# A four-layer transformer stack on one core: another layout of the rows stored in DRAM, and one order for the way into the output stage of both attention layers

## The chip, the core and the metric

The kernel runs on one core of a Trainium2 chip. The metric is the time of one execution on the device in microseconds, the median of several runs. TensorE multiplies matrices (PE in the profile; its weight loads, which overlap it, are PEld), VectorE is DVE, ScalarE is ACT, GpSimd is POOL. SyncE (SP) computes nothing: it issues the DMA transfers, one after the other. Weights and activations live in SBUF, sums of matmuls in PSUM, and what does not have to stay on the core goes to DRAM.

## The reference

Four layers on x of 2048 tokens by 576 features, in bfloat16: attention (A), MLP (B), A, B, each with a residual and a layer norm ahead of it.

```python
def _A_ref(x, wqkv, wo):
    H = 32; Dh = D // H                                  # 32 heads of 18
    qkv = (x @ wqkv).reshape(B, S, 3, H, Dh).transpose(2, 0, 3, 1, 4)
    q, k, v = qkv[0], qkv[1], qkv[2]
    phi = lambda t: jnp.where(t > 0, t + 1, jnp.exp(t)) + 1e-6
    pq, pk = phi(q), phi(k)
    kv = jnp.einsum("bhsd,bhse->bhde", pk, v)
    z = jnp.einsum("bhsd->bhd", pk)
    num = jnp.einsum("bhqd,bhde->bhqe", pq, kv)
    den = jnp.einsum("bhqd,bhd->bhq", pq, z)[..., None] + 1e-6
    o = num / den
    return o.transpose(0, 2, 1, 3).reshape(B, S, D) @ wo

def _B_ref(x, w1, b1, w2, b2):
    h = _gelu(jnp.einsum("bsd,df->bsf", _layernorm(x), w1) + b1)   # F = 4608
    return jnp.einsum("bsf,fd->bsd", h, w2) + b2

x = x + _A_ref(_layernorm(x), A_wqkv, A_wo)
x = x + _B_ref(_layernorm(x), B_w1, B_b1, B_w2, B_b2)
x = x + _A_ref(_layernorm(x), A_wqkv, A_wo)
x = x + _B_ref(_layernorm(x), B_w1, B_b1, B_w2, B_b2)
```

The attention is linear: keys and values are summed into one small matrix per head before any query is used.

## The kernel before

The tokens are worked on in 16 tiles of 128 rows (t), four tiles to a chunk of 512 (c, and j within the chunk). The 32 heads lie in five groups g of 126, 126, 126, 126 and 72 columns. yT holds the normed rows turned: features on partitions, tokens along the row. TensorE's order in the attention layers is the order of the program text (`pe` chains every matmul to the one before), and each other engine works its own instructions in the order that the scheduler gave them.

**Rows through DRAM.** In layer 1 (an MLP), each tile that is finished is normed for layer 2 and goes two ways. VectorE turns its 32 x 32 blocks into `turned` (L258), SP stores a chunk of four such tiles in four pieces to `y_d` (L266) and loads it back as columns of `yT` (`land`, L283 for the first 512 features, L286 for the last 64). And the row itself is stored in `yrow_d` (L406), because layer 2 also multiplies rows by keys. The turning leaves the tokens of a chunk in another order: block i of 32 rows of each of the four tiles j. A reload for "row" t = 4c + i therefore gathers 32 rows from each of four stored tiles: `load_row` (L251) for the first 512 columns, and L292 in `land` for the last 64 columns (the tails, four loads to a chunk, kept in `v_ring`). `yrow_d` has the shape [4 chunks, 4 tiles j, 4 blocks i, 32, 576], so that a stored tile is one contiguous piece and a reloaded row tile is four pieces of 32 rows. On SP's queue, the last chunk's steps are: four stores to `y_d`, the reloads of rows 6 to 11, the two loads of `yT`, four tail loads, the reloads of rows 12 to 15, and the residual rows of layer 2. A transfer that needs another's data, or its semaphore, is not issued before that has landed, and everything behind it on SP's queue waits too.

**Layer 2's keys.** For each tile and each half of the columns, `k_half` (L610) computes keys from `yT`, a `q_proj` follows every second of them (L589), and three steps behind, `rows_by_keys` (L627) multiplies the reloaded row by the keys.

**The way into the output stage (both attention layers).** Behind the sums, TensorE does these pieces:

- `q_proj(g, c)`, L589: five matmuls for the queries of one group and chunk. ACT then makes exp and a shifted copy of the result (L468, L469), and VectorE a min and a max (L476, L480). With `defer=True` these four are put off until the returned function is called.
- `kv_wo(g)`, L736: the small matrix of a group times wo, into a PSUM pair (accB for even g, accA for odd). ACT or VectorE copies it to SBUF (L743, L741).
- `den_stage(c)`, L752 and L756: the denominators of a chunk; VectorE takes the reciprocal (L760), and `quad_stage(c)` spreads it over a masked tile (L767).
- `scale_stage(g, c)`, L777: one matmul that broadcasts the reciprocals to a group's rows; ACT copies it to SBUF (L779) and VectorE multiplies the queries by it (L780).
- `wo_stage(t)`, L789: ten matmuls for one tile into accA or accB in turn, then `residual` (L519) adds and stores the row. For the first four tiles the layer norm of the MLP follows, with statistics on ACT (L337, L344) and a transpose on TensorE (L425) some tiles later.

PSUM has eight banks: four single ones in the pool `ps_h` (queries, denominators, broadcasts, transposes), and the pairs accA and accB. A piece that needs a bank waits until the last reader of what stood there is done.

The two layers enter the stage in different orders. Layer 0: kv_wo 0, a q_proj, denominators of chunks 0 and 1, q_proj, kv_wo 1, q_proj, broadcasts 0 to 2, kv_wo 2 and 3, broadcasts 3 and 4, kv_wo 4, q_proj. Layer 2 (its kv_wo 0 and 1 are done earlier): a q_proj, denominators of chunk 0, the values' matrices (`kv_groups`), q_proj, kv_wo 2 and 3, broadcasts 0 to 2, kv_wo 4, q_proj, broadcasts 3 and 4, denominators of chunk 1. In the loop over the tiles, each tile does `wo_stage`, the next chunk's broadcasts (three behind j = 0, two behind j = 1), then a q_proj if one is left, and then the denominators of the chunk after the next (behind j = 2 in layer 0, j = 1 in layer 2).

Of the kernel before, what the change touches and what calls it, by code (L numbers as in the profile page):

```python
# [9 lines left out]
BF16 = mybir.dt.bfloat16  # L10
# [24 lines left out]
def build(tc, A_x, A_wqkv, A_wo, B_w1, B_b1, B_w2, B_b2, out, dbg=None, n_layers=4):  # L35
    nc = tc.nc
    dbg = dbg or {}
    with ExitStack() as ctx:
# [77 lines left out]
        yrow_d = dpool.tile([NCB, TPC, 4, 32, D], BF16, name="yrow_d")  # L116
# [132 lines left out]
        def load_row(t):  # L249
            row_of[t] = blk.tile([P, D], BF16, name="yrow", tag="blk")  # L250
            load = nc.sync.dma_start(out=row_of[t][:, 0:4 * P], in_=yrow_d[t // TPC, :, t % TPC, :, 0:4 * P])  # L251
            if t >= 6:
                behind(load, "turned" if t < NT - TPC else "landed")
# [20 lines left out]
        def land(now=False):  # L274

            for it in list(landing):
# [11 lines left out]
                if kind == "A":  # L288
                    if c == NCB - 1:
                        sp_last["landed"] = landed.ins.name  # L290
                    for i in range(4):
                        tail = nc.sync.dma_start(out=tails(c)[:, i, 0:64], in_=yrow_d[c, :, i, :, 4 * P:D])  # L292
                        behind(tail, "landed")
                    if c == NCB - 1:
                        for t in range(c * TPC, NT):
                            load_row(t)
# [8 lines left out]
        class LNPipe:  # L305
# [11 lines left out]
            def tick(self, transposes=1):  # L317
                land()
                for it in list(self.items):
# [63 lines left out]
                    elif st in (2, 3):  # L383
# [20 lines left out]
                        if it["kind"] == "A" and it["evac"] == "dma":  # L404
                            c, j = divmod(it["t"], TPC)
                            nc.sync.dma_start(out=yrow_d[c, j].rearrange("i r d -> (i r) d"), in_=y[:, 0:D])  # L406
# [122 lines left out]
        def layer_A(li, next_kind, pre_a1=None):  # L529
# [203 lines left out]
            def kv_wo(g):  # L733
# [6 lines left out]
                if g % 2 or (li > 0 and g == 4):  # L740
# [7 lines left out]
            def den_stage(c, after=None):  # L748
                dp = ps_h.tile([P, 512], F32, name="den_ps", tag="h")
# [25 lines left out]
            def scale_stage(g, c):  # L775
                bp = ps_h.tile([P, 512], F32, name="rden_ps", tag="h")
                pe(nc.tensor.matmul(bp[:], lhsT=head_bc[:, g, :], rhs=quad_rden[c][:, 0:CA], start=True, stop=True))  # L777
# [22 lines left out]
            if li == 0:  # L800
                kv_wo(0)
                q_proj(*q_left.pop(0))
                den_stage(0)
                quad_stage(0)
                den_stage(1)
                quad_stage(1)
                q_proj(*q_left.pop(0))
                kv_wo(1)
                q_proj(*q_left.pop(0))
                for g in range(3):  # L810
                    scale_stage(g, 0)
                kv_wo(2)
                kv_wo(3)
                for g in range(3, G):
                    scale_stage(g, 0)
                kv_wo(4)
                q_proj(*q_left.pop(0))
            else:
                phi = q_proj(*q_left.pop(0), defer=True)
                den_stage(0)  # L820
                quad_stage(0)
                phi(dve_after=dve_last["quad"])
                kv_groups((2, 3, 4))
                late = [q_proj(*q_left.pop(0), defer=True)]
                kv_wo(2)
                kv_wo(3)
                for g in range(3):
                    scale_stage(g, 0)
                kv_wo(4)
                late.append(q_proj(*q_left.pop(0), defer=True))  # L830
                for g in range(3, G):
                    scale_stage(g, 0)
                den_stage(1, after=dve_last["mult"])
                quad_stage(1, after=dve_last["mult"])
                for phi in late:
                    phi(after=act_last["copy"])
            for t in range(NT):
# [4 lines left out]
                for late in list(rden_of):  # L842
                    quad_stage(late, after=dve_last["sum"])
                if c + 1 < NCA:
                    for g in ((0, 1, 2), (3, 4), (), ())[j]:
                        scale_stage(g, c + 1)
                if q_left:
                    q_proj(*q_left.pop(0))
                if j == (1 if li > 0 else 2) and c + 2 < NCA:
                    den_stage(c + 2)  # L850
# [242 lines left out]
```

## Time and profile before

| | |
|---|---|
| three runs | 772.51, 772.74, 774.62 us; median 772.74 |
| the profiled execution | 774.99 us, its span 773.3 us, mean granted clock of TensorE 0.998 |
| TensorE busy | 762.7 us (99%) |
| ACT, VectorE, GpSimd busy | 339.2, 273.7 and 119.4 us |
| layer 0, up to the first matmul of the MLP | to 108.65 us |
| layer 1, up to the first keys of layer 2 | 108.65 to 390.4 us |
| layer 2, up to the first matmul of the MLP | 390.4 to 488.0 us |
| layer 3 | 488.0 us to the end |
| first wo of layer 0, first wo of layer 2 | 80.15 and 460.54 us |

The span runs from the first to the last instruction of the profiled execution. Busy time of TensorE counts a matmul from its start to a modelled end, and neighbours overlap: the distance from one piece's start to the next one's start is what a piece costs. In the lists of waits, an engine and a line stand on the left, and what it waited for on the right. In the windows, the granted clock is the share of TensorE's full clock that the throttle let through, and the DMA share is the mean busy share of the 16 DMA engines.

### The profile page before, as it was taken

The numbers are of one execution on the slowest core, as the hardware profiler recorded it, in microseconds if no ns is written. First come the engines' busy times: TensorE is split into PE (matmuls) and PEld (weight loads), VectorE is DVE, ScalarE is ACT, GpSimd is POOL, SyncE is SP. The second block draws the span as 40 slices with busy tenths as digits, with TensorE's granted clock in tenths as the row PEclk, the third lists the DMA queues.
The fourth block names the chain that finished last, engine by engine and source line by source line (L and its number), as shares of the span: only waits on it lengthen the run. The fifth ranks groups of instructions, "written<-read, shape, count | busy, mean of one in ns | idle before, by whom it ended". The sixth has DMA issues, their size and how long they took to land.

```text
span 773.3 us, 15726 instructions
## 1 busy us (share of the span) xinstructions
PE 762.7 (99%) x6554; PEld 493.8 (64%) x6554; DVE 273.7 (35%) x676; ACT 339.2 (44%) x755; POOL 119.4 (15%) x196
## 2 busy tenths in 40 slices
PE   9999999999999999999998999999999999999998
PEld 6776664675477457646776767547745764675476
DVE  7786864035114503401354678610140023000000
ACT  5887846304610650263055568461065026205600
POOL 4571412011100301200100004210030002002000
PEclk9999999999999999999999999999999999999999
DMA  8991473015401631320147006730141033011000
GB/s 261 275 287 46 154 250 89 24 57 155 129 24 63 180 81 47 108 66 16 53 124 189 25 1 209 252 81 9 38 124 51 16 123 83 8 31 54 2 8 24
DMA packets 80290, 73.83 MB, mean 95 GB/s; under 512 B 36698, under 2 KB 64858, under 8 KB 80218
## 3 DMA queue, kind: packets, MB, share of 16 engines
q1 hardware_dynamic: 80218, 72.82, 32.4%
q8 instruction: 51, 0.84, 0.5%
q14 instruction: 21, 0.17, 0.1%
HBM read 48.03 MB, written 24.77 MB: 94 GB/s over the span
## 4 chain that ended last, share of the span: by engine, by line
PE 94%; DMA 2%; DVE 2%; ACT 1%; issue 1%; POOL 0%; SPq 0%; ACTq 0%
PE m_ps L974 35%; PE h_ps L917 20%; PE hp_ps L917 16%; PE q_ps L589 5%; PE wo_ps L789 4%; PE k_ps L541 2%; PE k_ps L610 2%; PE k_ps L627 2%; PE v_ps L562 1%; DMA yT<-y_d 1%; PE m_half L974 1%; PE v_ps L559 1%; PE tp L425 1%; PE rden_ps L777 1%; ACT rden_bc L779 1%
## 5 line engine op out<-in xcount | busy, mean ns | idle before, releaser
L974 PE MATMUL m_ps<-w_sb,hT 128*128 128x288 bf16 x2232 | 274.8, 286 | 0.0
L974 PEld LDWEIGHTS <-hT 128*128 128x128 bf16 x2304 | 224.8, 98 | 59.8 <-issue 3.4
L917 PEld LDWEIGHTS <-w_sb 64*128 64x128 bf16 x2304 | 124.5, 94 | 136.5 <-issue 1.9
L917 PE MATMUL hp_ps<-yT,w_sb 64*128 64x512 bf16 x1152 | 178.0, 376 | 0.0
L917 PE MATMUL h_ps<-yT,w_sb 64*128 64x512 bf16 x1152 | 148.0, 376 | 0.0
L922 ACT COPY relay_sb<-relay_sb 128x1 f32<-128x1 f32 x144 | 28.5, 198 | 262.6 <-PE h_ps L917 220.0
L913 ACT ACTIVATE hT<-h_ps,b1T 128x512 bf16<-128x512 f32 x144 | 91.0, 683 | 44.4 <-PE h_ps L917 44.4
L376 POOL TENSOR_TENSOR ln_rstd<-ln_u,neg_half 128x1 f32<-128x1 f32 x64 | 35.9, 562 | 376.6 <-DVE ln_u L367 229.5
L913 ACT ACTIVATE hT<-hp_ps,b1T 128x512 bf16<-128x512 f32 x144 | 91.1, 692 | 0.0
L519 DVE TENSOR_TENSOR xbf<-m_ps,xo 128x576 bf16<-128x576 f32 x15 | 11.4, 758 | 212.1 <-PE m_ps L974 212.1
L519 DVE TENSOR_TENSOR xo<-m_ps,xo 128x576 f32<-128x576 f32 x16 | 12.1, 758 | 167.2 <-PE m_ps L974 167.2
L502 POOL TENSOR_TENSOR xo<-xo,b_bc 128x576 f32<-128x576 f32 x32 | 41.0, 1286 | 106.1 <-DMA xo<-x_d 66.0
L917 PE MATMUL h_ps<-yT,w_tail 64*128 64x512 bf16 x144 | 54.1, 376 | 0.0
L917 PE MATMUL hp_ps<-yT,w_tail 64*128 64x512 bf16 x144 | 54.1, 376 | 0.0
L589 PE MATMUL q_ps<-yT,wqkv_sb 128*126 128x512 bf16 (+1 forms) x200 | 50.8, 386 | 0.1
L789 PE MATMUL wo_ps<-kvwo,pq 126*128 126x288 bf16 (+1 forms) x320 | 43.1, 285 | 0.2 <-DVE xo L519 0.2
L917 PEld LDWEIGHTS <-w_tail 64*128 64x128 bf16 x288 | 27.1, 94 | 17.1
L468 ACT ACTIVATE phi_e<-k_ps 128x288 bf16<-128x288 f32 x46 | 19.3, 421 | 41.2 <-PE k_ps L610 38.6
L789 PEld LDWEIGHTS <-pq 126*128 126x128 bf16 (+1 forms) x320 | 30.4, 97 | 10.2 <-issue 0.4
L476 DVE TENSOR_SCALAR phi_e<-phi_e 128x288 bf16<-128x288 bf16 (+2 forms) x86 | 24.1, 282 | 26.6 <-ACT phi_e L468 26.1
L589 PEld LDWEIGHTS <-wqkv_sb 128*126 128x126 bf16 (+1 forms) x200 | 25.3, 134 | 12.3 <-issue 0.8
L468 ACT ACTIVATE phi_e<-q_ps 126x512 bf16<-126x512 f32 (+1 forms) x40 | 23.8, 596 | 20.1 <-PE q_ps L589 19.9
(130 smaller groups left out, 666.2 us busy)
## 6 DMA issues: line engine op xcount, KB each, us to landing
xo<-x_d SPq DMA_DIRECT2D x48, 288.0 KB
x_d<-xo SPq DMA_DIRECT2D x32, 288.0 KB
xl<-x_d SPq DMA_DIRECT2D x24, 288.0 KB
y_d<-turned SPq DMA_DIRECT2D x40, 144.0 KB
w_sb<-in_B_w_dram SPq DMA_DIRECT2D x6, 864.0 KB
yT<-y_d SPq DMA_DIRECT2D x10, 512.0 KB
w_sb<-in_B_w_dram SPq DMA_DIRECT2D x9, 512.0 KB
x_d<-xn SPq DMA_DIRECT2D x16, 288.0 KB
```

The lines of the kernel that those rows point to most:

```text
L376: nc.gpsimd.tensor_tensor(out=rstd[:], in0=it["u"][:], in1=neg_half[:], op=ALU.pow)
L468: exp = nc.scalar.activation(out=e_out, in_=ps_ap, func=ACT.Exp)
L476: low = nc.vector.tensor_scalar(out=e[0:rows, 0:n], in0=e[0:rows, 0:n], scalar1=1.0, scalar2=1e-6, op0=ALU.min, op1=ALU.add)
L502: nc.gpsimd.tensor_tensor(out=xo[:], in0=xo[:], in1=b2_bc[:], op=ALU.add)
L519: total = nc.vector.tensor_tensor(out=xn[:, cols].rearrange("p (h n) -> p h n", h=2), in0=halves, in1=xo[:, cols].rearrange("p (h n) -> p ...
L541: pe(nc.tensor.matmul(kp[:, 0:HALF], lhsT=yT[:, k, tok], rhs=wqkv_sb[:, k, D + half * HALF: D + (half + 1) * HALF], start=(k == 0), stop=( ...
L589: pe(nc.tensor.matmul(qp[0:GR[g], :], lhsT=wqkv_sb[:, k, GO[g]:GO[g] + GR[g]], rhs=yT[:, k, c * CA:(c + 1) * CA], start=(k == 0), stop=(k ...
L789: pe(nc.tensor.matmul(wp[:, half, 0:HALF], lhsT=pq[(g, c)][0:GR[g], j * P:(j + 1) * P], rhs=kvwo[g][0:GR[g], half * HALF:(half + 1) * HALF ...
L913: act_last["gelu"] = nc.scalar.activation(out=to, in_=ps, func=ACT.Gelu_apprx_tanh, bias=b1T[:, f:f + 1], scale=1.0).ins.name
L917: mm = pe(nc.tensor.matmul(dst[n], lhsT=wt, rhs=mv, start=(seen[n] == 0), stop=(seen[n] == 8)))
L922: relay = nc.scalar.copy(out=relay_sb[:, 1:2], in_=relay_sb[:, 0:1])
L974: pe(nc.tensor.matmul(acc[half][:, 0:HALF], lhsT=hT[f][:, j * P:(j + 1) * P], rhs=w2_sb[:, f, half * HALF:(half + 1) * HALF], start=(f == ...
```

## The change

First, `yrow_d` has its two inner block dimensions exchanged: [chunks, blocks i, tiles j, 32, 576]. A reloaded row tile and a tail are then one run of 128 rows with one stride, so the four tail loads of a chunk become one, and a stored tile becomes four pieces of 32 rows.

Second, layer 0 takes layer 2's order, with kv_wo 0 and 1 ahead of it. In both layers the broadcast of group 3 moves ahead of the third q_proj and is written to accA, and the denominators of chunk 1 are written to accB; the second and third q_proj have their ACT and VectorE steps put off behind chunk 0's broadcasts. Layer 0 therefore does three q_proj ahead of the loop and three in it. In the loop a q_proj now stands ahead of the next chunk's broadcasts, and the denominators come behind j = 1 in both layers. In layer 0, kv_wo 4 is copied by VectorE, no longer by ACT. The broadcast's matmul keeps its 512 columns.

```diff
-        yrow_d = dpool.tile([NCB, TPC, 4, 32, D], BF16, name="yrow_d")
+        yrow_d = dpool.tile([NCB, 4, TPC, 32, D], BF16, name="yrow_d")
...
-            load = nc.sync.dma_start(out=row_of[t][:, 0:4 * P], in_=yrow_d[t // TPC, :, t % TPC, :, 0:4 * P])
+            load = nc.sync.dma_start(out=row_of[t][:, 0:4 * P], in_=yrow_d[t // TPC, t % TPC].rearrange("j r d -> (j r) d")[:, 0:4 * P])
...
-                    for i in range(4):
-                        tail = nc.sync.dma_start(out=tails(c)[:, i, 0:64], in_=yrow_d[c, :, i, :, 4 * P:D])
-                        behind(tail, "landed")
+                    tail = nc.sync.dma_start(out=tails(c)[:, :, 0:64],
+                                             in_=yrow_d[c].rearrange("i j r d -> (j r) i d")[:, :, 4 * P:D])
+                    behind(tail, "landed")
...
-                            nc.sync.dma_start(out=yrow_d[c, j].rearrange("i r d -> (i r) d"), in_=y[:, 0:D])
+                            nc.sync.dma_start(out=yrow_d[c, :, j], in_=y[:, 0:D])
...
-                if g % 2 or (li > 0 and g == 4):
+                if g % 2 or g == 4:
...
-            def den_stage(c, after=None):
-                dp = ps_h.tile([P, 512], F32, name="den_ps", tag="h")
+            def den_stage(c, after=None, pair=None):
+                if pair:
+                    dp = ps_acc.tile([P, 2, 512], F32, name="den_pair", tag=pair)[:, 0, :]
+                else:
+                    dp = ps_h.tile([P, 512], F32, name="den_ps", tag="h")
...
-            def scale_stage(g, c):
-                bp = ps_h.tile([P, 512], F32, name="rden_ps", tag="h")
-                pe(nc.tensor.matmul(bp[:], lhsT=head_bc[:, g, :], rhs=quad_rden[c][:, 0:CA], start=True, stop=True))
+            def scale_stage(g, c, pair=None):
+                if pair:
+                    bp = ps_acc.tile([P, 2, 512], F32, name="rden_pair", tag=pair)[:, 0, :]
+                else:
+                    bp = ps_h.tile([P, 512], F32, name="rden_ps", tag="h")
+                pe(nc.tensor.matmul(bp[:, 0:CA], lhsT=head_bc[:, g, :], rhs=quad_rden[c][:, 0:CA], start=True, stop=True))
...
             if li == 0:
                 kv_wo(0)
-                q_proj(*q_left.pop(0))
-                den_stage(0)
-                quad_stage(0)
-                den_stage(1)
-                quad_stage(1)
-                q_proj(*q_left.pop(0))
                 kv_wo(1)
-                q_proj(*q_left.pop(0))
-                for g in range(3):
-                    scale_stage(g, 0)
-                kv_wo(2)
-                kv_wo(3)
-                for g in range(3, G):
-                    scale_stage(g, 0)
-                kv_wo(4)
-                q_proj(*q_left.pop(0))
-            else:
-                phi = q_proj(*q_left.pop(0), defer=True)
-                den_stage(0)
-                quad_stage(0)
-                phi(dve_after=dve_last["quad"])
+            phi = q_proj(*q_left.pop(0), defer=True)
+            den_stage(0)
+            quad_stage(0)
+            phi(dve_after=dve_last["quad"])
+            if li > 0:
                 kv_groups((2, 3, 4))
                 late = [q_proj(*q_left.pop(0), defer=True)]
-                kv_wo(2)
-                kv_wo(3)
-                for g in range(3):
-                    scale_stage(g, 0)
-                kv_wo(4)
-                late.append(q_proj(*q_left.pop(0), defer=True))
-                for g in range(3, G):
-                    scale_stage(g, 0)
-                den_stage(1, after=dve_last["mult"])
-                quad_stage(1, after=dve_last["mult"])
-                for phi in late:
-                    phi(after=act_last["copy"])
+            kv_wo(2)
+            kv_wo(3)
+            if li == 0:
+                late = [q_proj(*q_left.pop(0), defer=True)]
+            for g in range(3):
+                scale_stage(g, 0)
+            kv_wo(4)
+            scale_stage(3, 0, pair="accA")
+            late.append(q_proj(*q_left.pop(0), defer=True))
+            scale_stage(4, 0)
+            den_stage(1, after=dve_last["mult"], pair="accB")
+            quad_stage(1, after=dve_last["mult"])
+            for phi in late:
+                phi(after=act_last["copy"])
             for t in range(NT):
...
+                if q_left:
+                    q_proj(*q_left.pop(0))
                 if c + 1 < NCA:
                     for g in ((0, 1, 2), (3, 4), (), ())[j]:
                         scale_stage(g, c + 1)
-                if q_left:
-                    q_proj(*q_left.pop(0))
-                if j == (1 if li > 0 else 2) and c + 2 < NCA:
+                if j == 1 and c + 2 < NCA:
                     den_stage(c + 2)
```

## The prediction

> **What bounds the kernel now.** I read the page first, then who waits for whom on TensorE, then the stretch of the longest wait on SP's queue, by windows, and last the two entries into the output stage, on TensorE's timeline.
>
> ```profile
> PE 762.7 (99%) x6554; PEld 493.8 (64%) x6554; DVE 273.7 (35%) x676; ACT 339.2 (44%) x755; POOL 119.4 (15%) x196
> ```
>
> TensorE runs 762.7 of 773.3 us and the change takes no matmul away. What it can win lies in the 10.6 us of idle time and in matmuls that ran at a lower clock. TensorE's own waits (who waited for whom: total, times, longest):
>
> ```profile
> PE k_ps L610 <- DMA yT<-y_d: 2.5, 1, 2.5
> ...
> PE rden_ps L777 <- DVE quad_rden L767: 1.1, 3, 0.5
> PE kvwo_ps L736 <- ACT kvwo L743: 0.7, 1, 0.7
> PE kvwo_ps L736 <- DVE kvwo L741: 0.6, 1, 0.6
> PE den_ps L752 <- ACT rden_bc L779: 0.5, 1, 0.5
> ```
>
> The first is where layer 2 begins: keys of the last 512 tokens wait for their turned rows. The other four lie in the output stages of layers 0 and 2, which the change reorders. First SP's queue before that first wait (start, duration, instruction), then windows (length, busy time of each engine, granted clock, DMA share, GB/s):
>
> ```profile
> 394.65 0.32 SPq L406 DMA_DIRECT2D yrow_d<-y_ring  x1
> 395.54 2.44 SPq L266 DMA_DIRECT2D y_d<-turned  x4
> 398.09 5.13 SPq L251 DMA_DIRECT2D yrow<-yrow_d  x6
> 403.31 1.30 SPq L283 DMA_DIRECT2D yT<-y_d  x1
> 404.66 1.38 SPq L286 DMA_DIRECT2D yT<-y_d  x1
> 406.09 4.87 SPq L292 DMA_DIRECT2D v_ring<-yrow_d  x4
> ```
>
> ```profile
> 86.00:92.00 6.00, 5.84 (x66) 4.00 (x64) 4.47 (x9) 6.00 (x17) 4.16 (x9) 1.00 0.59 197
> 401.00:404.00 3.00, 3.00 (x23) 2.21 (x21) 0.97 (x4) 1.82 (x5) 0.00 (x0) 1.00 0.27 93
> 406.00:407.00 1.00, 1.00 (x10) 0.81 (x9) 0.40 (x2) 0.85 (x2) 0.00 (x0) 1.00 1.08 328
> 413.00:415.00 2.00, 2.00 (x12) 1.40 (x11) 0.54 (x2) 0.71 (x2) 0.00 (x0) 0.61 0.23 62
> 415.00:417.00 2.00, 2.00 (x6) 1.10 (x6) 0.54 (x2) 0.71 (x2) 0.00 (x0) 0.53 0.89 240
> 417.00:420.00 3.00, 3.00 (x24) 2.37 (x23) 1.26 (x4) 2.13 (x6) 0.00 (x0) 1.00 1.06 240
> ```
>
> Two things are to be seen. While only row reloads (L251) are in flight (401 to 404), the DMA engines are 0.27 busy at 93 GB/s, about 4.3 of 16 engines; while yT<-y_d adds its packets (406 to 407) it is 1.08 and 328 GB/s. So the reload of a [4, 32]-strided source keeps four engines busy, and yT, queued behind it, waits on those four. And after the 2.52 us wait the granted clock was 0.61 and 0.53 for 4 us: a second cost of 2 x 0.39 + 2 x 0.47 = 1.72 us.
>
> Last, the four entry waits on TensorE's timeline (idle before and its releaser in brackets):
>
> ```profile
> 77.32 0.41 PE L736 MATMUL kvwo_ps<-wo_sb,kvT 126*126 126x288 bf16 x2 [0.64 <-DVE kvwo L741]
> ...
> 78.82 0.41 PE L736 MATMUL kvwo_ps<-wo_sb,kvT 72*72 72x288 bf16 x2 [0.67 <-ACT kvwo L743]
> ```
>
> ```profile
> 460.08 0.47 PE L752 MATMUL den_ps<-pq,zsel 126*32 126x128 bf16 x20 [0.46 <-ACT rden_bc L779]
> ...
> 462.36 0.82 PE L777 MATMUL rden_ps<-quad_rden,head_bc 128*128 128x512 bf16 x3 [0.42 <-DVE quad_rden L767]
> ```
>
> **The change, part 1: layout of the stored rows.** The reload's source becomes 128 rows with one stride. I take it that it then spreads as yT<-y_d does. Six loads of 128 KB are 768 KB: 8.4 us at 93 GB/s, 2.4 us at 328. The first six reloads then no longer hold four engines for 8.4 us, and the six in front of yT drain about as fast as SP issues them. Their issue falls from 5.13 us to about 6 x 0.60 (0.51 us, the shortest of them, plus the semaphore step) = 3.6 us, so yT<-y_d goes out at 398.09 + 3.6 = 401.7 instead of 403.31. It asks for the four y_d<-turned stores, issued by 398.0; its other conditions were met before. L283 and L286 carry 576 KB: 1.8 us at 328 GB/s, and with some 2 us around it, as from the issue at 403.31 to the full rate at 406, yT lands near 406 to 407. The keys need it at 409.89 (412.41 - 2.52). Slack 3 us: the wait goes, and with it the drop of the clock: **-2.52 - 1.72 = -4.24 us**. What is late next: rows 12 to 15 and their 64-column tails. The four tail loads (4.87 us of SP) become one with the same 128-byte pieces, between 1.3 (one of the four) and 4.87 us; then four reloads, 2.4 us. They are issued by 407 to 411 and used from about 415.7 (six half-steps of 0.6 to 1.1 us behind 409.89). Hidden.
>
> The price is on the other side: the store (L406, 16 of them) now writes [4, 32, 576]. If four engines carry it, 144 KB take 144/93 = 1.6 us instead of 0.4. Fifteen of them lie under second matmuls of layer 1, where TensorE waits for no DMA; the last goes out 0.9 us ahead of y_d<-turned and delays its share on four engines by at most 1.6 us, inside the 3 us. Zero, at most 1.6.
>
> [...] No run yet shows that store.
>
> **Part 2: the entry of layer 0** takes layer 2's order: two kv_wo first, one q_proj, denominators of chunk 0, kv_wo 2 and 3, q_proj, broadcasts; chunk 1's denominators behind chunk 0's broadcasts; three q_proj instead of four ahead of the loop. Steps from the timeline: q_proj 1.08 us, kv_wo 0.25, denominators 0.45, three broadcasts 0.65, two 0.43, wo 1.23, engine latency behind TensorE 0.2. From 71.06: kv_wo(1) 71.30, q 72.38, den 72.83, two kv_wo 73.33, q 74.41. The reciprocal (0.95) starts at 73.40 behind the q's first DVE step, the quad is done at 74.82: a new wait of 0.47. Broadcasts to 75.53, kv_wo(4) 75.78, the copy of kv_wo(3) frees accA at 75.85, broadcast 3 to 76.13, q 77.21, broadcast 4 to 77.43, den in accB 77.88, wo(0). Its fifth group waits for ACT's copy (77.63 to 78.22) and DVE's product (78.64): wo(0) ends at 79.44, with the q_proj that was put off at 80.52, where before both were done at 81.38. The 0.64 and 0.67 are gone, 0.47 and 0.33 come: -0.86. Walking on in this way, chunk 2's broadcasts end at 89.8 (before 91.09), those of chunk 3 at 97.5 (before 98.64), since den comes one tile earlier and its quad is no longer late; about 0.85 of new waits there stand behind ACT, which computes the statistics. Sum **-1.15 us**.
>
> **Part 3: the entry of layer 2.** den(1) in accB no longer waits for a broadcast's bank (0.46), and a q_proj stands ahead of the broadcasts that waited for the quad (0.42). wo(0) then waits 0.34 for its last product: it ends at 461.37 (before 461.77), q and broadcasts at 463.10 (before 464.10). Then wo(4) waits 0.6 for the sum of tile 2, which stands on DVE behind products that ACT's statistics hold up; at den(3) the lead is 0.4. **-0.45 us**.
>
> Bounds of parts 2 and 3: all entry waits gone and none new, 0.64 + 0.67 + 1.1 + 0.46 + 0.2 = -3.1; every new wait of the walk (0.47, 0.33, 0.85, 0.34, 0.6) without its gain, +2.6 in place of -1.6, which the -0.86 and -0.40 already reached at the two wo(0) make unlikely; I keep +1. I take -1.6, nearer the walk than either end.
>
> **Sum.** 774.99 - 4.24 - 1.6 = 769.15 for the profiled execution (span 773.3, so 1.7 around it). It stands 2.25 above the median of the three, 772.74; these are 772.51, 772.74 and 774.62. The 1.9 between two and one is near the 1.72 of the clock drop, so I take it that the two lower runs had the wait without the drop. Then the median falls by 2.52 + 1.6 to 768.6; if they had it too, to 766.9. I forecast 768.4.
>
> [...]
>
> **Rivals.** (a) The entries give nothing: the new waits eat the 1.6. For it: ACT is busy 6.00 of 6.00 us from 86 to 92. Against it: the lead at both wo(0). 770.2 without the clock drop in the runs, 768.5 with it. (b) yT lands as late as before: the reload doesn't spread, or the store on four engines holds y_d. For it: only a share of 0.27 stands for the spreading, and issue times near 1.3 us show a queue that pushes back. Against: 3 us of slack. Only the entries are left: 771.1, within the noise. (c) Slower: ACT becomes the bound of the output stages. Three q_proj fall into layer 0's loop instead of two, and two put-off ones enter it with four activations of 0.49 us each; at 86 to 92 ACT has no free time. If all 6 x 0.49 = 2.9 us land on wo in layer 0, and in layer 2 the 0.98 of the q_proj that now stands ahead of the broadcasts, on top of the 0.85 and 0.6 of the walk, 5.3 are lost against the 2.52: 775.5. It decides once ACT, not TensorE, ends each step from wo(1) to wo(8).
>
> **Chances.** Forecast 0.63, (a) 0.18, (b) 0.13, (c) 0.06. A measurement of this kernel tells 0.3% (2.3 us) from no change: under 770.4 is faster, over 775.1 slower. Forecast and most of (a) are faster, 0.78; (b) and the rest of (a) are the same, 0.16; (c) is slower, 0.06. Low end of the range: 772.74 - 4.24 - 3.1 = 765.4; high end 771.3, which takes in (a) and (b).
>
> **What would show it.** yT<-y_d is issued near 402 and lands by 407; TensorE has no wait on it at L610, and no window of layer 2 has a clock under 1; the reload's windows exceed 200 GB/s. A wait at L610 over 1 us refutes part 1; a first wo of layer 0 that ends after 80.3 refutes part 2; wo_ps waiting for DVE or ACT for more than 2 us in all would be (c).

## The result and the profile after

Four executions of the changed kernel took 768.49, 767.98, 768.62 and 768.38 us, median 768.43. Four of the kernel before, measured beside them, took 772.74, 772.51, 774.62 and 774.49, median 773.62. The ratio is 0.9932, 95% interval 0.9914 to 0.9951. The profiled execution took 768.49 us, its span is 766.8 us, the mean granted clock 1.000.

First the busy times, from the page of the changed kernel, and then what TensorE waited for (who waited for whom: total us, times, longest). Line numbers have moved a little: the broadcast is now L783, wo L795, the spread L770.

```profile
PE 760.5 (99%) x6554; PEld 492.8 (64%) x6554; DVE 273.3 (36%) x677; ACT 338.6 (44%) x754; POOL 120.5 (16%) x196
```

```profile
PE warm_ps L177 <- DVE y_ring L172: 1.3, 1, 1.3
PE k_ps L541 <- DMA wqkv_sb<-in_A_wqkv_dram: 0.5, 1, 0.5
PE rden_ps L783 <- DVE quad_rden L770: 0.2, 1, 0.2
PE wo_ps L795 <- DVE xo L519: 0.2, 1, 0.2
PE rden_ps L783 <- ACT rden_bc L785: 0.2, 1, 0.2
```

The wait on `yT<-y_d`, 2.5 us before, is not there, and none of the four entry waits is left; the 0.2 us at the quad is a new wait, in layer 0. The first two lines are the start of the kernel, which the change does not touch. TensorE's busy time fell by 2.2 us with the same 6554 matmuls: fewer of them ran at a lower clock (a mean granted clock of 0.998 before, 1.000 after).

SP's queue ahead of the keys of tile 12 (start, duration, instruction), and the windows of that stretch (length, busy time of PE, PEld, DVE, ACT and POOL, granted clock, DMA share, GB/s):

```profile
394.10 3.24 SPq L266 DMA_DIRECT2D y_d<-turned  x4
397.44 4.01 SPq L251 DMA_DIRECT2D yrow<-yrow_d  x6
401.55 0.38 SPq L283 DMA_DIRECT2D yT<-y_d  x1
401.98 0.52 SPq L286 DMA_DIRECT2D yT<-y_d  x1
402.55 0.57 SPq L291 DMA_DIRECT2D v_ring<-yrow_d  x1
403.24 1.86 SPq L251 DMA_DIRECT2D yrow<-yrow_d  x4
```

```profile
400.00:404.00 4.00, 4.00 (x29) 2.86 (x28) 2.17 (x8) 2.95 (x8) 0.00 (x0) 1.00 0.79 211
404.00:408.00 4.00, 4.00 (x30) 2.97 (x29) 1.88 (x7) 2.63 (x7) 0.00 (x0) 1.00 1.07 314
408.00:412.00 4.00, 4.00 (x31) 3.02 (x30) 2.04 (x7) 2.98 (x8) 0.00 (x0) 1.00 0.98 299
```

`yT<-y_d` goes out at 401.55 in place of 403.31, but layer 2 itself begins 1.44 us earlier (its first key at 388.94, before at 390.38), so that within the layer the issue moved by only 0.3 us. Its two issues take 0.90 us in place of 2.68, and TensorE is busy 4.00 of 4.00 us at a clock of 1.00 where it had stood.

TensorE at the entry of layer 0 (start, duration; idle before and its releaser in brackets):

```profile
74.64 0.81 PE L783 MATMUL rden_ps<-quad_rden,head_bc 128*128 128x512 bf16 x3 [0.23 <-DVE quad_rden L770]
...
77.69 1.70 PE L795 MATMUL wo_ps<-kvwo,pq 126*128 126x288 bf16 x10
79.23 1.24 PE L589 MATMUL q_ps<-yT,wqkv_sb 128*126 128x512 bf16 x5
80.31 0.81 PE L783 MATMUL rden_ps<-quad_rden,head_bc 128*128 128x512 bf16 x3
```

The 0.23 is the new wait at the quad. The first wo takes 1.54 us to the start of the next piece, where another takes 1.23: the rest is a wait inside it for the last group's queries. It begins at 77.69, before at 80.15 (behind one q_proj more).

To see where the time went, all profiled executions of this study are cut at the same five points of TensorE's timeline: z_ps of layer 0, first h_ps of layer 1, first k_ps of layer 2, z_ps of layer 2, first h_ps of layer 3. The rows of the experiments are explained below.

| lengths in us | start to z | layer 0, z to MLP | layer 1 | layer 2, keys to z | layer 2, z to MLP | layer 3 |
|---|---|---|---|---|---|---|
| before | 70.44 | 38.21 | 281.73 | 62.06 | 35.54 | 285.32 |
| after | 70.13 | 37.08 | 281.73 | 57.68 | 35.16 | 285.02 |
| after, second profile | 69.63 | 37.07 | 281.74 | 57.68 | 35.15 | 285.03 |
| layout alone | 70.14 | 37.69 | 281.74 | 57.69 | 35.54 | 285.00 |
| order alone | 70.41 | 37.09 | 281.74 | 61.53 | 35.16 | 285.37 |
| after, source padded | 69.94 | 37.08 | 281.74 | 60.62 | 35.16 | 285.36 |
| before, yT ahead of four reloads | 69.87 | 37.69 | 281.74 | 57.69 | 35.54 | 285.27 |
| before, filler | 70.01 | 38.20 | 281.74 | 59.86 | 35.53 | 285.26 |
| before, reloads in four loads | 69.54 | 38.20 | 281.73 | 65.23 | 35.54 | 284.96 |
| after, no borrowed banks | 70.19 | 37.41 | 281.73 | 57.69 | 35.55 | 285.03 |
| after, nothing put off | 70.25 | 38.18 | 281.74 | 57.68 | 36.91 | 285.04 |
| after, old order in the loop | 69.86 | 38.18 | 281.73 | 57.69 | 35.13 | 285.01 |

The profiled executions of before and after differ by 6.5 us: 4.38 in layer 2's keys, 1.13 and 0.38 in the two output stages, none in layer 1, and 0.31 + 0.30 in the start and in layer 3. The start is not the change: that column moves by up to 0.9 us among all kernels, with no relation to the edit. Layer 3 is another matter. It has two lengths, 285.3 us in the five kernels that reload a row tile by one load of [4, 32] rows and 285.0 in the other seven, and the 0.3 lies behind the last matmul, where SP has a gap of 0.3 us among the program's closing instructions. It goes with the form of the reload; why, no run shows.

### The profile page after: what moved, and what is told of

It reads as the page before. It is cut to its first block, busy times and chain, and to the rows that moved or that the text cites. A ratio compares the mean times of both kernels' runs of the same rounds, so it can differ in the third digit from the quotient of the medians.

```text
span 766.8 us, 15710 instructions
## 1 busy us (share of the span) xinstructions
PE 760.5 (99%) x6554; PEld 492.8 (64%) x6554; DVE 273.3 (36%) x677; ACT 338.6 (44%) x754; POOL 120.5 (16%) x196
## 4 chain that ended last, share of the span: by engine, by line
PE 95%; ACT 3%; DVE 1%; DMA 1%; issue 1%; SPq 0%; DVEq 0%; ACTq 0%
PE m_ps L967 36%; PE h_ps L910 20%; PE hp_ps L910 16%; PE q_ps L589 5%; PE wo_ps L795 3%; PE k_ps L541 3%; PE k_ps L610 3%; PE k_ps L627 2%; PE v_ps L562 1%; PE m_half L967 1%; PE v_ps L559 1%; ACT rden_bc L785 1%; PE tp L425 1%; DMA wqkv_sb<-in_A_wqkv_dram 1%; ACT ln_dump L337 1%; PE kvacc L583 1%
## 5 line engine op out<-in xcount | busy, mean ns | idle before, releaser
L795 PE MATMUL wo_ps<-kvwo,pq 126*128 126x288 bf16 (+1 forms) x320 | 43.7, 286 | 0.6 <-DVE xo L519 0.2
L795 PEld LDWEIGHTS <-pq 126*128 126x128 bf16 (+1 forms) x320 | 30.1, 97 | 11.1 <-DVE pq L786 0.8
```

What stands on the lines that cost most here:

```text
L795: pe(nc.tensor.matmul(wp[:, half, 0:HALF], lhsT=pq[(g, c)][0:GR[g], j * P:(j + 1) * P], rhs=kvwo[g][0:GR[g], half * HALF:(half + 1) * HALF ...
```

## The experiments

Each execution is listed with its mean granted clock, and this turned out to matter. Of the 23 executions of the kernel before that stood beside the first four experiments, 14 have a clock of 1.000 and a median of 772.18 us, 9 have 0.998 and a median of 773.71. Where a kernel shows both kinds, like is compared with like below.

**Each half of the change alone.** Layout alone is the kernel before with the first four hunks of the diff:

```diff
-        yrow_d = dpool.tile([NCB, TPC, 4, 32, D], BF16, name="yrow_d")
+        yrow_d = dpool.tile([NCB, 4, TPC, 32, D], BF16, name="yrow_d")
...
```

> The kernel before with the new layout of the stored rows alone (both layers keep their old way into the output stage). Theory (layout): yT<-y_d is issued near 401.7 and lands before the keys need it, the wait of 2.5 us at k_ps and the clock drop behind it are gone, and layer 2's first keys come at the same time as before; 2.5 to 4.2 us less than the kernel before, near 770.0 us. Rival (the change's gain in layer 2 comes from its new order): the wait stays, no change within 1 us. Rival (four-engine stores cost something): the wait is gone but layer 1 is longer than 281.7 us or the last y_d store lands late, 0.5 to 1.6 us of the gain are missing.

It took 769.41 us (768.97 to 769.62, all with a clock of 1.000), ratio to before 0.9953 (0.9941 to 0.9964). Its windows:

```profile
400.00:404.00 4.00, 4.00 (x30) 2.98 (x29) 1.97 (x8) 2.66 (x8) 0.00 (x0) 1.00 0.77 190
404.00:408.00 4.00, 4.00 (x29) 2.89 (x28) 1.94 (x7) 2.97 (x8) 0.00 (x0) 1.00 1.03 298
```

The wait and the drop are gone, keys to z take 57.69 us as in the changed kernel, and layer 1 is the 281.74 us that it is everywhere, so the stores on [4, 32, 576] cost TensorE nothing (what they cost the queue is told further below). Both rivals fall.

Order alone is the changed kernel with these four hunks taken back.

> The changed kernel with the old layout of the stored rows (its new order into the output stage alone). Theory: the wait of about 2.5 us at k_ps on yT<-y_d remains, with a clock below 1 behind it in at least some executions; the output stages bring 1.6 us, of it 1.15 in layer 0 and 0.45 in layer 2, so about 771.0 to 772.0 us. Rival (the entries give nothing): same as before, wait included. Rival (the entries carry the change): below 770 us although the wait is there.

It took 772.79 us (771.05 to 773.46, 11 executions), ratio 0.9995 (0.9986 to 1.0004). TensorE's timeline and its windows:

```profile
410.73 0.79 PE L610 MATMUL k_ps<-wqkv_sb,yT 128*128 128x288 bf16 x5 [1.99 <-DMA yT<-y_d]
```

```profile
408.00:412.00 4.00, 2.01 (x17) 1.40 (x16) 1.03 (x4) 1.53 (x4) 0.00 (x0) 1.00 0.29 72
412.00:416.00 4.00, 4.00 (x18) 2.45 (x16) 1.08 (x4) 1.48 (x5) 0.00 (x0) 0.57 0.58 174
```

The wait is there, and behind it the clock falls to 0.57 for 4 us. Eight of 11 executions had the drop, 9 of 23 of the kernel before, so the medians mix two things. Like with like, the order is worth 0.93 us without the drop (772.18 to 771.25) and 0.82 with it (773.71 to 772.89). So neither of the theory's figures, 1.6 us, nor the rival's nothing: the gain of the order is about 0.9.

**What makes the reload slow.** In the old layout a reload's source is four pieces of 32 rows far apart. Is it the distance, or the factor 4 in the shape? One empty row behind each piece keeps the pieces next to each other and the shape at [4, 32]:

```diff
-        yrow_d = dpool.tile([NCB, 4, TPC, 32, D], BF16, name="yrow_d")
+        yrow_d = dpool.tile([NCB, 4, TPC, 33, D], BF16, name="yrow_d")
...
-... in_=yrow_d[t // TPC, t % TPC].rearrange("j r d -> (j r) d")[:, 0:4 * P])
+... in_=yrow_d[t // TPC, t % TPC][:, 0:32, 0:4 * P])
...
```

The store and the tails, four loads to a chunk again, follow this shape.

> The changed kernel with one empty row behind each piece of 32 stored rows, and four tail loads again. A reload's source is then as near to contiguous as in the changed kernel (gaps of 1,152 bytes), but it is [4, 32] and no longer one run of 128 rows. Theory (number of engines, the factor 4 in the shape): the reloads keep about four engines busy again, DMA share near 0.27 and some 93 GB/s while they are alone in flight, and the wait at k_ps is back with 2 to 3 us: the time of the kernel with the new order alone, within 0.5 us. Rival (contiguous addresses make the reload fast): no wait, the time of the changed kernel, 768.4 us.

772.78 us (771.54 to 775.06, 12 executions), ratio 1.0001 (0.999 to 1.0013): all that the layout gives is lost. SP's queue, TensorE and the windows of this kernel:

```profile
397.27 4.80 SPq L251 DMA_DIRECT2D yrow<-yrow_d  x6
402.17 1.30 SPq L283 DMA_DIRECT2D yT<-y_d  x1
403.52 1.38 SPq L286 DMA_DIRECT2D yT<-y_d  x1
```

```profile
411.02 0.79 PE L610 MATMUL k_ps<-wqkv_sb,yT 128*128 128x288 bf16 x5 [2.76 <-DMA yT<-y_d]
```

```profile
408.00:410.00 2.00, 0.26 (x3) 0.00 (x0) 0.77 (x3) 0.77 (x2) 0.00 (x0) 1.00 0.27 93
410.00:412.00 2.00, 0.98 (x8) 0.81 (x9) 0.00 (x0) 0.15 (x1) 0.00 (x0) 1.00 0.29 51
412.00:414.00 2.00, 2.00 (x15) 1.42 (x13) 0.92 (x4) 1.27 (x4) 0.00 (x0) 1.00 0.26 80
```

The issues of `yT<-y_d` are back at 1.30 and 1.38 us, and from 408 to 410 the DMA engines have a share of 0.27 at 93 GB/s, as in the kernel before. While only reloads go out, from 400 to 402, it is 0.26 and 90 GB/s; in the changed kernel, from 400.0 to 401.5, it is 0.79 and 215. A gap of one row is enough: it is the shape, not the distance. This profiled execution also shows the wait without the drop: 2.76 us of idling and a clock of 1.00 right behind it.

The other way about: can the old layout spread, if each reload is issued as four loads of 32 rows?

```diff
-            load = nc.sync.dma_start(out=row_of[t][:, 0:4 * P], in_=yrow_d[t // TPC, :, t % TPC, :, 0:4 * P])
+            for j in range(4):
+                load = nc.sync.dma_start(out=row_of[t][32 * j:32 * (j + 1), 0:4 * P],
+                                         in_=yrow_d[t // TPC, j, t % TPC, :, 0:4 * P])
...
```

> The kernel before with its old layout, but each reload of a row tile as four loads of 32 contiguous rows, so that each load spreads by its 32 rows; SP issues 64 loads for 16. Theory (number of engines that one load uses): while reloads alone are in flight the DMA share is over 0.5 and the rate over 150 GB/s; what the wait then is depends on SP: 24 issues ahead of yT at 0.3 us and more are over 7 us in place of 5.1, so that yT goes out at 405 or later and the wait stays at 1 to 4 us. Rival (the strided addresses are slow in themselves): DMA share near 0.27 as before, 93 GB/s, and a longer wait.

776.95 us (776.78 to 778.11), ratio 1.0049 (1.0036 to 1.0062), slower. All five executions have the drop; against the kernel before with the drop (774.10 beside this one) it is 2.9 us more. SP's queue and the windows:

```profile
397.23 12.84 SPq L252 DMA_DIRECT2D yrow<-yrow_d  x24
410.11 0.43 SPq L285 DMA_DIRECT2D yT<-y_d  x1
```

```profile
400.00:408.00 8.00, 8.00 (x57) 5.82 (x56) 3.88 (x14) 5.69 (x14) 0.00 (x0) 1.00 0.27 65
408.00:412.00 4.00, 0.97 (x7) 0.49 (x5) 1.03 (x3) 1.12 (x3) 0.00 (x0) 0.97 0.31 79
412.00:416.00 4.00, 1.74 (x8) 1.15 (x9) 0.00 (x0) 0.32 (x2) 0.00 (x0) 0.50 0.54 162
```

24 issues took 12.84 us, 0.53 each; at 32 KB per issue that is 61 GB/s, and the window shows 65 for all traffic: SP is the limit, `yT<-y_d` goes out at 410.11, and the wait is 5.3 us, beyond the 1 to 4 that were expected. The rate that was expected (over 150 GB/s) could not come about, so this run tells nothing of how a single load spreads; that a load of 32 rows spreads was the author's estimate and is not shown. It tells that small loads are no way out: keys to z take 65.23 us.

**Bytes ahead in the queue.** If yT only waits on what the reloads ahead of it still have to move, it is enough to put it ahead of that, with the layout as it was:

```diff
...
-                for row in range(6, NT - TPC):
+                for row in range(6, 8):
                     load_row(row)
...
                         sp_last["landed"] = landed.ins.name
+                        for t in range(8, NT - TPC):
+                            load_row(t)
```

> The kernel before with its old layout, but on SP's queue the reloads of rows 8 to 11 stand behind the two loads of yT and ahead of the tails, so that only two slow reloads are ahead of yT in place of six. Theory (yT waits on the four engines behind the bytes queued ahead of it): yT<-y_d is issued near 399.5 and lands by 405, the wait at k_ps and the clock drop are gone, rows 8 to 11 (needed from about 408 on, 1.6 us apart) land from 404 on in time: 2.5 to 4.2 us less than the kernel before, the same time as the layout alone within 0.5 us. Rival (the wait is moved to the rows): rows_by_keys waits for yrow or the tails by 1 us or more, and the gain is below 1.5 us. Rival (the load of yT is itself slow): the wait stays above 1 us.

769.93 us (769.5 to 770.27, all at 1.000), ratio 0.9959 (0.9948 to 0.9971). Its queue:

```profile
397.01 1.63 SPq L251 DMA_DIRECT2D yrow<-yrow_d  x2
400.72 0.38 SPq L283 DMA_DIRECT2D yT<-y_d  x1
401.15 0.51 SPq L286 DMA_DIRECT2D yT<-y_d  x1
401.76 2.40 SPq L251 DMA_DIRECT2D yrow<-yrow_d  x4
```

Keys to z take 57.69 us, the same as with the new layout, and no wait has moved to the rows. The theory holds but for the issue, which is at 400.72 and not 399.5: between 398.64 and there SP waits 1.9 us for the stores to `y_d` to land, which `yT<-y_d` reads. So two edits, one of shape and one of place in a queue, each take the whole wait away. The medians differ by 0.5 us; 0.3 of it is the end of the program, where this kernel still has the 285.3 us of the old reloads, and the rest is open.

**Wait and clock drop apart.** Ten matmuls whose sum is never read fill the place where TensorE waits in the kernel before:

```diff
+                    if half == 0 and t == NT - TPC:
+                        fill_ps = ps_h.tile([P, 512], F32, name="fill_ps", tag="h")
+                        for _ in range(10):
+                            pe(nc.tensor.matmul(fill_ps[:], lhsT=wqkv_sb[:, 0, 0:P], rhs=yT[:, 0, 0:512],
+                                                start=True, stop=True))
```

> The kernel before with ten matmuls more (128x512 on weights and turned rows that are long there, some 2.2 us, the sum never read) ahead of the keys of tile 12, so that TensorE works where it otherwise waits for yT<-y_d. Theory (the drop of the clock is a cost of its own, paid for idling): no execution has a mean granted clock under 0.9985, and the time is that of those executions of the kernel before that have no drop, 772.2 within 0.7 us, at least 1.2 below those that have it (773.7); the wait left at k_ps is under 0.7 us. Rival (the drop comes from something else at that place, as the rate at which rows and keys alternate): about four executions in ten still have it. Rival (the filler costs as much as it hides): 774 or more.

772.64 us (772.09 to 773.15), and all 11 executions have a clock of 1.000. Beside it stood 15 executions of the kernel before: six without the drop, median 772.49, nine with it, median 774.10. So the filler costs what the wait costs, and takes away the drop, which is worth 1.6 us by itself. The windows of the filler:

```profile
408.00:410.00 2.00, 2.00 (x13) 1.24 (x12) 0.85 (x4) 1.59 (x4) 0.00 (x0) 1.00 0.27 94
410.00:412.00 2.00, 2.00 (x13) 0.97 (x12) 0.41 (x1) 0.00 (x0) 0.00 (x0) 1.00 0.31 72
412.00:416.00 4.00, 4.00 (x31) 3.04 (x30) 1.69 (x6) 2.71 (x7) 0.00 (x0) 1.00 0.48 128
```

VectorE and ACT run dry from 410 to 412, as in a wait, but TensorE is busy, and the clock stays at 1.00. Both rivals fall.

**The parts of the new order.** The changed kernel once more, for the size of the terms:

> The changed kernel once more, beside the three others on one chip and with a second profile, for the size of the terms. Theory (the layout carries all but 0.9 of it): 768.4 us within 0.5; all executions at a mean granted clock of 1.000; from z_ps to the first matmul of the MLP 37.1 us in layer 0 and 35.2 in layer 2, from the first keys to z_ps 57.7 us. Rival (the entries bring the predicted 1.6): 1.6 us or more below the kernel with the layout alone (769.41), 767.8 or less.

768.71 us (767.99 to 768.77); one execution of the five shows 0.999, the others 1.000. The stages are those of the theory. The kernel with the layout alone ran on another chip, where the kernel before at a clock of 1.000 took 772.18 us, against 772.49 beside this one. So the order is worth 769.41 - 768.71 + 0.31 = 1.0 us on top of the layout, which the stages confirm (37.69 - 37.07 and 35.54 - 35.15). The rival's 767.8 is not reached.

Then one part of the order was taken back at a time. The borrowed banks:

```diff
-            scale_stage(3, 0, pair="accA")
+            scale_stage(3, 0)
...
-            den_stage(1, after=dve_last["mult"], pair="accB")
+            den_stage(1, after=dve_last["mult"])
```

> The changed kernel without the borrowed banks: the broadcast of group 3 and the denominators of chunk 1 take a bank of the common four again. Theory (the borrowed banks are what spares den(1) its wait): TensorE waits 0.3 to 0.5 us once in each of the two entries for a bank that ACT has to empty, 0.3 to 0.9 us more than the changed kernel. Rival (the order alone does it, the banks are free by then): the same time within 0.2 us.

769.29 us (768.94 to 769.41), 0.6 more than the changed kernel beside it; the stages say 0.34 in layer 0 and 0.40 in layer 2. The size is as expected, the place is not. TensorE's timeline in layer 0:

```profile
75.75 0.38 PE L783 MATMUL rden_ps<-quad_rden,head_bc 128*128 128x512 bf16 x1
76.24 1.24 PE L589 MATMUL q_ps<-yT,wqkv_sb 128*126 128x512 bf16 x5
```

From group 3's broadcast to the q_proj behind it are 0.49 us, in the changed kernel 0.21. It is the q_proj that finds no bank, not the denominators of chunk 1.

The second steps of the queries, no longer put off:

```diff
-                late = [q_proj(*q_left.pop(0), defer=True)]
+                q_proj(*q_left.pop(0))
...
-            late.append(q_proj(*q_left.pop(0), defer=True))
+            q_proj(*q_left.pop(0))
...
```

> The changed kernel in which the second and third q_proj of each entry run their ACT and VectorE steps at once instead of behind chunk 0's broadcasts. Theory (putting them off keeps ACT and VectorE free for the copies and products that the first wo needs): the first wo of each layer waits for its last products, 0.5 to 2 us more in each entry (four ACT steps of 0.49 us each stand ahead), 1 to 3 us in all: 769.7 to 771.7 us. Rival (ACT and VectorE have room there): the time of the changed kernel, 768.6 within 0.4 us.

771.40 us (771.21 to 771.80), 2.7 more than the changed kernel: 1.11 in layer 0 and 1.76 in layer 2, so that layer 2's stage is 1.37 us longer than in the kernel before. TensorE, then ACT, of this kernel in layer 0:

```profile
79.56 0.91 PE L795 MATMUL wo_ps<-kvwo,pq 72*128 72x288 bf16 x6 [0.77 <-DVE pq L786]
```

```profile
77.43 0.67 ACT L468 ACTIVATE phi_e<-q_ps 126x512 bf16<-126x512 f32 x1
77.92 0.67 ACT L469 ACTIVATE phi_a<-q_ps 126x512 bf16<-126x512 f32 x1
78.39 0.62 ACT L785 CAST rden_bc<-rden_ps 72x512 bf16<-72x512 f32 x1
```

and the same copy in the changed kernel:

```profile
77.39 0.58 ACT L785 CAST rden_bc<-rden_ps 72x512 bf16<-72x512 f32 x1 [0.29 <-issue]
```

One q_proj's two activations stand ahead of the last copy, which starts at 78.39 in place of 77.39; the last product and the first wo stand behind it. In layer 2 a kv_wo waits as well, 0.56 us for ACT's copy of an earlier one, ahead of the 0.83 us of the first wo.

The order in the loop, as it was before:

```diff
-                if q_left:
-                    q_proj(*q_left.pop(0))
                 if c + 1 < NCA:
                     for g in ((0, 1, 2), (3, 4), (), ())[j]:
                         scale_stage(g, c + 1)
-                if j == 1 and c + 2 < NCA:
+                if q_left:
+                    q_proj(*q_left.pop(0))
+                if j == (1 if li > 0 else 2) and c + 2 < NCA:
```

> The changed kernel with the old order inside the loop over the tiles (a q_proj behind the next chunk's broadcasts; layer 0's denominators behind j = 2 again) and the new entries. Theory (of the walk in the prediction: half of layer 0's gain comes in the loop, since the denominators come one tile earlier and their quad is no longer late): from z_ps to the first matmul of the MLP layer 0 takes 37.3 to 37.7 us in place of 37.08, TensorE waits again for quad_rden at the broadcasts of chunks 2 or 3, by 0.2 to 0.5 us each; layer 2 unchanged at 35.16: 0.2 to 0.6 us in all. Rival (the loop's order brings nothing): 37.1 and 35.2, the time of the changed kernel within 0.2 us.

769.48 us (769.32 to 769.67), 0.8 more than the changed kernel; layer 0 takes 38.18 us, layer 2 is unchanged at 35.13. What TensorE waits for:

```profile
PE rden_ps L783 <- DVE quad_rden L770: 1.9, 5, 0.6
```

Three of the five, 0.42, 0.60 and 0.24 us, are the broadcasts of chunks 1, 2 and 3 in layer 0. The fourth, 0.23, is there in the changed kernel too, and the fifth, in layer 2, does not lengthen its stage. The loss in layer 0's stage is 1.10 us in this profile, nearly twice the upper figure of the theory, which had not counted chunk 1: with the q_proj behind the broadcasts, nothing covers the quad of chunk 1 either, whose denominators the new entry puts later.

The three parts don't add up. Without the deferral or without the loop's order, layer 0 takes 38.18 us, about what it took before; only all of them together give 37.08.

## Why the prediction was right

The predicted time was 768.4 us, the range 765.4 to 771.3; measured were 768.43 and, in a second set, 768.71. By its steps:

**Part 1, the reload.** Right in mechanism, and shown from three sides: the layout alone removes the wait, a factor 4 in the shape alone brings it back, and moving yT ahead of four of the slow reloads removes it with the old layout. Its times are another matter. The issue of six reloads was put at 3.6 us and took 4.01. yT was to go out at 401.7 and did at 401.55, but that agreement is luck: 401.7 was counted on the old timeline, in which layer 2 begins 1.44 us later. Counted from layer 2's first key, yT goes out 12.6 us in, before 12.9, and the prediction had 11.3. What moved is the landing. Before, the keys got yT 9.1 us behind its first issue (at 412.41); now SP's wait for that load (L497, the last line below) ends 4.7 us behind the issue, 17.3 us in, and in the second profile the second load has landed 17.7 us in. The keys start 19.3 us in, so the slack is about 1.6 us and not 3. What SP waited for within the 4.01 us, and then behind the loads of yT, in the changed kernel:

```profile
SPq L251 <- ACT phi_a L469: 2.0, 3, 1.2
SPq L251 <- ACT phi_e L468: 0.4, 1, 0.4
SPq L251 <- PE q_ps L589: 0.2, 1, 0.2
...
SPq L497 <- DMA yT<-y_d: 0.6, 1, 0.6
```

An issue takes 0.38 us (that of yT), not 0.60; 2.6 us of the 4.01 are waits for a buffer that ACT and TensorE still read. The same waits stood in the 5.13 us before, with 2.2 us. The buffers now set when the reloads go out: without these waits the six issues take 1.4 us, where before they took 2.9. In the windows, reloads of [4, 32] rows alone in flight go at 93 GB/s and a share of 0.27 with their pieces far apart, and at 90 GB/s and 0.26 with the pieces close together; with 128 rows in one run, the two loads of yT behind the six reloads are issued in 0.90 us in place of 2.68, and the windows show 211 and 314 GB/s at shares of 0.79 and 1.07. The "four engines" are an estimate from the share alone, 0.27 x 16 = 4.3; how many engines one load uses, no run shows.

**The term of 4.24 us.** It measured 4.38 between the two profiled executions, and is two costs, as the prediction had it. In executions without the drop, the layout alone is worth 772.18 - 769.41 = 2.77 us; 2.52 were predicted for the wait, and 0.3 of the 2.77 is the end of the program. The drop is 1.53 by the first group of runs of the kernel before (773.71 - 772.18), 1.61 by the second, and 1.8 by a third, which stood beside the last two experiments (11 executions, seven with the drop); 1.72 were predicted. That the two lower runs of the kernel before had the wait without the drop was inferred from three times; the clocks of these 49 executions bear the picture out, with two kinds of run 1.5 to 1.8 us apart.

**The stores on [4, 32, 576].** "Zero, at most 1.6" was zero for TensorE: layer 1 takes 281.73 to 281.74 us in every kernel. For the queue it was 0.8 us. SP needs 0.52 us to issue the last of these stores, 0.32 before, and the four stores to `y_d` behind it take 3.24 us in place of 2.44, so that the reloads start 8.5 us behind layer 2's first key and not 7.7. The slack hides this. In the padded kernel, which stores in four pieces too but has no slack, it shows: yT goes out 13.4 us behind that key, 12.6 with the order alone, and the wait is 2.76 us, 1.99 with the order alone. The 1.6 us was put on four engines for this store at the reload's 93 GB/s; no run shows this, and what the runs show in its place is the 0.8 us of the queue.

**Parts 2 and 3, the entries.** This is the term that was mis-sized: -1.6 predicted, -0.9 to -1.0 measured. Layer 2 is right (0.38 against 0.45), and on the predicted way: counted from z_ps, its first wo ends 0.39 us earlier than before, 0.40 predicted. In layer 0 the q_proj behind the first wo ends 0.76 us earlier, 0.86 predicted. The waits that the walk names for this add up to no more than 0.64 + 0.67 - 0.47 - 0.33 = 0.51; the new ones came out smaller, at 0.23 and 0.31, which makes 0.77. All in all, layer 0's -1.15 matches the profiled pair (1.13), but the old order has two lengths there. In the profile of the kernel before, the broadcasts of chunk 3 waited 0.52 us for a late quad, and the walk booked this as a wait that the new order removes. Two other profiles with the same old order, layout alone and yT moved ahead, have no such wait, and their stage is 37.69 us long: against them the order brings 0.6, which with layer 2's 0.4 makes 1.0, near the 0.9 to 1.0 of the medians. Two more have it, with the filler and with split reloads (38.20). What goes with it is told in the last section; how often executions without a profile have it is not known. Of the new waits of the walk, the quad cost 0.23 in place of 0.47, what stands behind the statistics on ACT 0.2 in place of 0.85, and the wo(4) of layer 2 0.2 in place of 0.6. As the walk said, the earlier denominators matter: with the old loop order the gain of layer 0 is gone.

**The sum.** Without the drop, the layout brought 0.25 us more than was predicted for the wait, and the entries some 0.65 less. From the kernel before without the drop (772.18 and 772.49 on the two chips), 2.77 + 0.93 lead to 768.5 and 768.8. That the forecast came within 0.1 us of the first median is partly errors that cancelled.

**The rivals.** (a) needed the entries to give nothing: order alone is 0.8 to 0.9 us faster, like with like. (b) needed yT to land as late as before: it does not. (c), ACT as the bound, did not come about, but the run with nothing put off shows a case of it: two activations ahead of one copy, and the first wo of layer 0 waits 0.77 us, in layer 2 0.83. The deferral is what keeps it away.

## What to carry to other kernels

In this kernel a transfer's cost hung on the shape it is written in: 128 rows as [4, 32] with gaps went at 93 GB/s, as one run of 128 rows they no longer held up the queue, and what suffered was the transfer behind them (two issues in 2.68 us, in place of 0.90). Where such a shape can't be had, look at the order of the queue first: moving one needed load ahead of slow ones that have time took the whole wait of 2.5 us away without a change of layout, while cutting the loads smaller made SP's issue the bound (24 issues in 12.84 us).

Times of one event in two profiles are compared from the start of its stage, or a shift that was won elsewhere is taken for a gain. Here a wait of TensorE of 2.5 us cost 1.5 to 1.8 us more than its length, and not in each execution: keep the granted clock of every run beside its time before comparing medians. And a wait in one profile is one sample: before it is booked as a gain, see whether it stands in a second profile of the same code.

## What the runs showed of the hardware

**The wait and the clock drop.** In the profile of the kernel before, the granted clock is 0.50 for one stretch of 3.41 us, from 413.46 on; in the 3.41 us ahead of it TensorE stood idle for 2.36 us. With the order alone, the clock is 0.50 from 412 to 414 and 0.65 from 414 to 416, behind a wait of 1.99 us: some 3.4 us at 0.50 (an estimate from these two windows). With split reloads it is 0.93, 0.50, 0.50, 0.50 and 0.86 in the five windows of 2 us from 410 on, some 6.8 us at 0.50 (an estimate in the same way); there the wait is 5.3 us, the drop begins within it, and all five executions of that kernel have a mean clock of 0.998 or less. The wait of the padded kernel, 2.76 us, is longer than those of the first two, 2.52 and 1.99 us, and the clock behind it stayed at 1.00. So the length of the wait alone does not decide; eight of the 11 executions with the order alone had the drop, and 9 of the first 23 of the kernel before. What decides, no run shows. A stretch of 3.41 us at half clock is a loss of up to 1.7 us (an estimate, 3.41 x 0.5), near the 1.5 to 1.8 of the medians.

**An accident between VectorE and GpSimd.** The spread of the reciprocals for chunk 3 in layer 0 meets a normalisation on GpSimd. First the kernel before, then the layout alone (start, duration):

```profile
97.00 0.93 DVE L767 TENSOR_TENSOR quad_rden<-quad_mask,rden 128x512 bf16<-128x512 bf16 x1
```

```profile
96.84 0.82 POOL L393 TENSOR_SCALAR y_ring<-xn,ln_rstd,ln_nmr 128x576 bf16<-128x576 f32 x1
```

```profile
96.70 0.42 DVE L767 TENSOR_TENSOR quad_rden<-quad_mask,rden 128x512 bf16<-128x512 bf16 x1
```

```profile
96.56 1.09 POOL L393 TENSOR_SCALAR y_ring<-xn,ln_rstd,ln_nmr 128x576 bf16<-128x576 f32 x1
```

Either VectorE takes 0.93 us for what takes 0.42 elsewhere, or GpSimd 1.09 for what takes 0.82: one of the two takes longer. In the three profiles with the spread of 0.93 us (before, with the filler, with split reloads) GpSimd takes 0.82 and started 0.16 us ahead; in the two with the spread of 0.42 and 0.41 (layout alone, yT moved ahead) it takes 1.09 and 1.10 and started 0.14 and 0.15 ahead. That each holds up the other is the author's reading of these durations: GpSimd's recorded start is the earlier one in all five, and no run here took the GpSimd instruction away to show the cause. In the new order no spread is over 0.43 us in the profile after.
